# Dense FFN moved from the routed tiles into the attention loop of a fused attention and mixture-of-experts kernel

## The chip, the core and the metric

The kernel runs on one core of one Trainium2 chip. A core has a matrix engine (TensorE, PE in the profile), a vector engine (VectorE, DVE), a scalar engine (ScalarE, ACT), a general engine (GpSimd, POOL) and a synchronising engine (SyncE, SP) that here only issues DMAs. Each engine runs its own instructions in their order and waits on semaphores for the others. Data moves between device memory and the on-chip memory SBUF by DMA; matrix products land in PSUM. The metric is device time in microseconds of one execution.

## The reference

```python
def _attn_ref(q, k, v, g_q, g_k):            # q, k, v: (8, 12, 448, 64)
    q_n, k_n = rmsnorm(q, g_q), rmsnorm(k, g_k)
    scores = (1/8) * q_n @ k_n^T
    attn = softmax(scores)                    # over the last axis
    return attn @ v

def _moe_ref(x, w_gate, w1_dense, w2_dense, w1, w2):   # x: (3584, 768)
    y_dense = maximum(x @ w1_dense, 0) @ w2_dense       # 768 -> 512 -> 768
    logits = x @ w_gate                                 # 8 experts
    e = argmax(logits); gate = softmax(logits)[e]
    y_moe = gate * (maximum(x @ w1[e], 0) @ w2[e])      # one expert per row
    return y_dense + y_moe
```

The attention output of the 8 batches, with its 12 heads side by side, is x: 3584 rows of 768. Every row goes through the dense FFN and through one of eight expert FFNs of the same size.

## The kernel before

The program has two stages and a planning part between them.

**First stage.** It loops over 48 tiles t; a tile is two heads of one batch, so six tiles make a batch. Two tiles make a group g; the q and k of a group are loaded by SP (`load`, L132, three buffers each) and its v by POOL (`load_v`, L140, two buffers, converted to bf16 on the way). For a tile, POOL squares q and k (`sq`, L151), DVE sums the squares (`ssq`, L152), ACT turns a group's sums into factors (L158, L159), DVE multiplies (`y`, L167), PE transposes (L177), DVE copies the transposes out of PSUM (L182, L184), PE makes the scores (L193), ACT takes their exponentials (`ex`, L195, four of them to a tile), PE multiplies with v (`attend`, L206), DVE divides (`divide`, L214, L219), PE transposes the result (L227) and ACT copies it (L229). After a batch's sixth tile `route` (L238 to L259) makes its logits, its one-hot choice and its gate, and SP writes a record of each row to device memory: x in bf16 and the gate. Squares are made four tiles ahead, normalised values three ahead, scores one ahead.

A buffer of q or k is free for the load of group g when the second tile of group g-3 has been multiplied on DVE; so SP's load waits for DVE (L167), POOL's square waits for the load, and DVE's sum waits for POOL.

The weights come by DMAs that POOL issues: two for the dense FFN with group 1 and two for each expert with every second group from the fourth on (`norm_ahead`). DMAs that POOL issues share one queue.

**Planning** (L305 to L390). From the one-hot choices, DVE and PE work out where each row stands when rows are sorted by expert, each expert's rows padded to whole tiles of 128: 35 slot tiles.

**Second stage.** For each slot tile, POOL gathers 128 records by an indirect DMA (L397, two tiles ahead), PE transposes x (L407), multiplies with the expert's w1 (L414) and with the dense w1 (L420), ACT applies the two relus (L416 with the gate, L423), PE transposes the expert's hidden values (L426) and multiplies the dense ones (L432) and the expert's (L436) with their w2 into one PSUM tile, DVE copies it (L440) and POOL scatters 128 rows of 3,072 bytes to the output by an indirect DMA (L441). A scatter waits for the one before it to have landed, since both write the output.

The order on each engine is set by a scheduler that places instructions as it expects them to become ready; the source order is only its input.

Of the kernel before, what the change touches and what calls it, by code (L numbers as in the profile page):

```python
# [8 lines left out]
F32 = mybir.dt.float32  # L9
# [8 lines left out]
def kernel(  # L18
# [86 lines left out]
    xd = nc.dram_tensor("x_rows", (N, RW // 2), F32).ap()  # L105
    oh = const.tile([P, B, 4, E], BF16)
    wgb = const.tile([P, KD, E], BF16)
    nc.gpsimd.dma_start(wgb, moe_w_gate.rearrange("(ko p) e -> p ko e", p=P))
# [4 lines left out]
    def load_weights(dst1, dst2, s1, s2):  # L113
        nc.gpsimd.dma_start(dst1, s1.rearrange("(ko p) f -> p ko f", p=P))
        nc.gpsimd.dma_start(dst2, s2.rearrange("(fo p) d -> p fo d", p=P))

    def load_expert(dst, e):
        load_weights(dst[:, 0].rearrange("p (ko f) -> p ko f", f=F),
                     dst[:, 1].rearrange("p (fo d) -> p fo d", d=Dm), moe_w1[e], moe_w2[e])

    with tc.tile_pool(name="a_ld", bufs=3) as ld, \
         tc.tile_pool(name="a_sb", bufs=2) as sb, \
         tc.tile_pool(name="a_sc", bufs=2, space=bass.MemoryType.PSUM) as scp, \
         tc.tile_pool(name="a_av", bufs=1, space=bass.MemoryType.PSUM) as avp, \
         tc.tile_pool(name="a_tr", bufs=2, space=bass.MemoryType.PSUM) as trp:
        xin, ssqs, rs, xn, qkT, exs, vas, xnats, xTs = {}, {}, {}, {}, {}, {}, {}, {}, {}

        def load(g):
            b, h0 = divmod(g * GP * 2, H)
            for name, src in (("q", q), ("k", k)):  # L130
                t = ld.tile([SC, 2 * GP, JJ * D], F32, tag="x" + name)
                nc.sync.dma_start(  # L132
                    t, src[b, h0:h0 + 2 * GP].rearrange("h (p j) d -> p h (j d)", j=JJ))
                xin[name, g] = t
            ssqs[g] = sb.tile([SC, 2, 2 * GP * JJ], F32, tag="ssq", name="ssq")

        def load_v(g):
            b, h0 = divmod(g * GP * 2, H)
            vr = ld.tile([SC, 2 * GP, JJ * D], BF16, tag="vr", bufs=2)
            nc.gpsimd.dma_start(vr, v[b, h0:h0 + 2 * GP].rearrange("h (p j) d -> p h (j d)", j=JJ))  # L140
            va = ld.tile([SC, 2 * GP, JJ, D + 2], BF16, tag="va")
            nc.vector.memset(va[:, :, :, D:], 1.0)
            nc.vector.tensor_copy(va[:, :, :, :D], vr.rearrange("p h (j d) -> p h j d", d=D))  # L143
            vas[g] = va

        def squares(t):
            g, i = divmod(t, GP)
            for n, name in enumerate("qk"):
# [5 lines left out]
                    sq.rearrange("p h (j d) -> p (h j) d", d=D), AX.X, ALU.add)  # L154

        def rnorm(g):
            r = sb.tile([SC, 2, 2 * GP * JJ], F32, tag="r", name="r")
            nc.scalar.activation(r, ssqs[g], AF.Ln, bias=eps_t[:SC], scale=1.0 / D)  # L158
            nc.scalar.activation(r, r, AF.Exp, scale=-0.5)  # L159
            rs[g] = r  # L160

        def normalise(t):
            g, i = divmod(t, GP)
            for n, name in enumerate("qk"):
# [8 lines left out]
        def transposes(t):  # L173
            for name in "qk":
                ps = trp.tile([P, S], BF16, tag="tr")
                for j in range(JJ):
                    nc.tensor.transpose(ps[:, j * SC:(j + 1) * SC],  # L177
                                        xn[name, t][:, j].rearrange("p h d -> p (h d)"),
                                        ident[:SC, :SC])
                y = sb.tile([P, S], BF16, tag="T" + name)  # L180
                if name == "q":
                    nc.vector.tensor_scalar(y, ps, gqk, None, op0=ALU.mult)  # L182
                else:
                    nc.vector.tensor_copy(y, ps)  # L184
                qkT[name, t] = y
# [296 lines left out]
```

## Time and profile before

| | |
|---|---|
| median of three runs | 606.62 us (598.64, 606.62, 606.91) |
| profiled execution | 599.36 us, span 597.7 us, mean granted TensorE clock 0.838 |
| PE busy | 443.1 us, 74% of the span |
| DVE busy | 311.6 us, 52% |
| ACT busy | 247.4 us, 41% |
| POOL busy | 205.7 us, 34% |
| chain that ended last | DMA 31%, issue 26%, PE 17%, DVE 15% |

The span is from the first to the last instruction. The granted clock is the share of 2.4 GHz that TensorE was given: 1.00 is 2.4 GHz and 0.50 is 1.2 GHz; a mean between them is a mixture. A busy share is an average over stages that have different limits, so the rows below are taken by stage.

### The profile page before, as it was taken

Reading aid. Unit: us, or ns where it says so; the run is one execution under the profiler, and the core shown is the slowest. Engines: PE = TensorE matmul, PEld = TensorE weight load, DVE = VectorE, ACT = ScalarE, POOL = GpSimd, SP = SyncE. Lnnn points to the kernel's source line nnn. Section 1 sums busy time; section 2 is a strip of 40 time slices with the busy share of each in tenths; the row PEclk is TensorE's granted clock in tenths of the full one; section 3 lists DMA queues with packets and bytes.
Section 4 is the critical chain, followed back from the end, with each engine's and each line's share of the span. In section 5 each row is a group of like instructions: output and inputs, shape, how many; then the busy total and the mean of one; then the engine's idle time right before and its main releaser. Section 6 shows DMA issues by size and latency. Waiting matters only on the chain.

```text
span 597.7 us, 11804 instructions
## 1 busy us (share of the span) xinstructions
PE 443.1 (74%) x4682; PEld 294.6 (49%) x4682; DVE 311.6 (52%) x666; ACT 247.4 (41%) x367; POOL 205.7 (34%) x223
## 2 busy tenths in 40 slices
PE   0558766679986697689781058888889888888895
PEld 0335444445554465456450046556656565555663
DVE  4589976678778768776645513223232322223231
ACT  0447774566676677667780002111121122111220
POOL 5567654336344333542000022222322233222321
PEclk9998985575587858855995559999999999999999
DMA  8999999993654365443101012222122122222210
GB/s 174 222 157 237 239 250 225 230 237 80 148 130 125 82 137 139 78 124 78 47 3 47 0 41 82 71 80 80 64 86 91 65 81 93 90 80 73 81 63 1
DMA packets 55253, 65.89 MB, mean 110 GB/s; under 512 B 4365, under 2 KB 51725, under 8 KB 55200
## 3 DMA queue, kind: packets, MB, share of 16 engines
q0 software_dynamic: 28768, 37.59, 30.2%
q1 hardware_dynamic: 26432, 27.54, 16.5%
q8 instruction: 39, 0.64, 0.4%
q14 instruction: 14, 0.11, 0.1%
HBM read 68.27 MB, written 19.28 MB: 146 GB/s over the span
## 4 chain that ended last, share of the span: by engine, by line
DMA 31%; issue 26%; PE 17%; DVE 15%; POOL 4%; ACT 4%; SPq 1%; POOLq 0%; DVEq 0%; ACTq 0%
DMA out_dram<-ys,dest 16%; DMA vr<-in_v_dram 7%; PE av L206 7%; DMA t<-in_k_dram 5%; PE ps L193 5%; DVE y L167 4%; ACT ex L195 4%; POOL sq L151 3%; PE ps L177 2%; DVE xa L219 2%; DMA t<-in_q_dram 2%; DVE ssq L152 2%; PE ps L227 2%; DVE va L143 1%; POOL xg L397 1%
## 5 line engine op out<-in xcount | busy, mean ns | idle before, releaser
L195 ACT ACTIVATE ex<-ps 112x896 bf16<-112x896 f32 x192 | 168.9, 918 | 67.7 <-PE ps L193 66.5
L151 POOL TENSOR_TENSOR sq<-t 112x512 f32<-112x512 f32 x96 | 101.5, 1074 | 109.1 <-DMA t<-in_q_dram 56.3
L193 PE MATMUL ps<-y 64*112 64x448 bf16 x384 | 98.3, 493 | 41.9 <-DVE y L184 25.9
L206 PEld LDWEIGHTS <-ex 112*128 112x128 bf16 x1536 | 73.6, 114 | 70.8 <-issue 40.4
L206 PE MATMUL av<-va,ex 112*128 112x65 bf16 x1536 | 93.8, 220 | 18.1 <-DVE xa L219 18.0
L416 ACT ACTIVATE hs<-he,xg 128x512 bf16<-128x512 f32 x35 | 24.1, 687 | 183.0 <-PE he L414 183.0
L441 POOL DMA_INDIRECT out_dram<-ys,dest x35 | 35.5, 1016 | 158.7 <-DVE ys L440 158.7
L167 DVE TENSOR_TENSOR y<-t,r 112x512 bf16<-112x512 f32 x96 | 78.7, 843 | 1.6 <-ACT r L159 1.6
L152 DVE TENSOR_REDUCE ssq<-sq 112x8 f32<-112x512 f32 x96 | 62.9, 675 | 26.8 <-POOL sq L151 26.8
L440 DVE COPY ys<-yp 128x768 f32<-128x768 f32 x35 | 33.5, 958 | 77.4 <-PE yp L436 77.4
L432 PE MATMUL yp<-wd,hdT 128*128 128x384 bf16 x280 | 51.6, 327 | 25.8 <-ACT hdT L423 20.0
L397 POOL DMA_INDIRECT xg<-x_rows,row x35 | 34.2, 977 | 86.3 <-DVE dest L390 70.6
L193 PEld LDWEIGHTS <-y 64*112 64x112 bf16 x384 | 30.3, 148 | 64.3 <-DVE y L184 29.4
L177 PE MATMUL ps<-ident,y 112*128 112x112 bf16 x384 | 40.1, 262 | 26.9 <-DVE y L167 24.6
L428 DVE COPY heT<-hp 128x512 bf16<-128x512 bf16 x35 | 14.9, 425 | 85.1 <-PE xp L407 71.5
L420 PEld LDWEIGHTS <-wd 128*128 128x128 bf16 x840 | 51.1, 99 | 8.6 <-issue 0.6
L420 PE MATMUL hd<-xT,wd 128*128 128x128 bf16 x840 | 53.9, 222 | 0.0
L414 PE MATMUL he<-we,xT 128*128 x210 | 52.3, 386 | 0.8 <-DVE xT L409 0.8
L436 PE MATMUL yp<-we,heT 128*128 x280 | 51.2, 326 | 0.0
L432 PEld LDWEIGHTS <-hdT 128*128 128x128 bf16 x280 | 24.5, 98 | 45.3 <-ACT hdT L423 24.6
L177 PEld LDWEIGHTS <-y 112*128 112x128 bf16 x384 | 30.1, 124 | 29.7 <-DVE y L167 25.3
L423 ACT ACTIVATE hdT<-hd 128x512 bf16<-128x512 f32 x35 | 20.9, 597 | 43.3 <-PE xp L407 38.9
(95 smaller groups left out, 392.8 us busy)
## 6 DMA issues: line engine op xcount, KB each, us to landing
we<-in_moe_w_dram POOLq DMA_DIRECT2D x16, 768.0 KB, 29.1
t<-in_q_dram SPq DMA_DIRECT2D x24, 448.0 KB, 5.9
t<-in_k_dram SPq DMA_DIRECT2D x24, 448.0 KB, 7.0
vr<-in_v_dram POOLq DMA_DIRECT2D x24, 224.0 KB, 6.7
x_rows<-xa SPq DMA_DIRECT2D x8, 577.5 KB, 3.7
wd<-in_moe_w_dense_dram POOLq DMA_DIRECT2D x2, 768.0 KB, 10.1
x_rows<-xa SPq DMA_DIRECT2D x8, 96.2 KB, 3.6
xg<-x_rows,row POOLq DMA_INDIRECT x35, 3.1
```

The costliest lines, as they stand in the source:

```text
L151: nc.gpsimd.tensor_mul(sq, x, x)
L152: nc.vector.tensor_reduce(ssqs[g][:, n, 2 * i * JJ:(2 * i + 2) * JJ], sq.rearrange("p h (j d) -> p (h j) d", d=D), AX.X, ALU.add)
L167: nc.vector.tensor_mul(y.rearrange("p j h d -> p h j d"), x.rearrange("p h (j d) -> p h j d", d=D), rs[g][:, n, 2 * i * JJ:(2 * i + 2) * J ...
L177: nc.tensor.transpose(ps[:, j * SC:(j + 1) * SC], xn[name, t][:, j].rearrange("p h d -> p (h d)"), ident[:SC, :SC])
L193: nc.tensor.matmul(ps[:, hh, :S], qkT["k", t][d0:d0 + D, j * SC:(j + 1) * SC], qkT["q", t][d0:d0 + D, :], start=True, stop=True)
L195: nc.scalar.activation(exs[t][:, j], ps[:, :, :S], AF.Exp, scale=scale)
L206: nc.tensor.matmul(av[t][:, hh, mi * De:(mi + 1) * De], exs[t][:, j, hh, QC[mi]:QC[mi] + P], vas[t // GP][:, 2 * (pr % GP) + hh, j, :De], ...
L397: nc.gpsimd.indirect_dma_start(out=xg, out_offset=None, in_=xd, in_offset=bass.IndirectOffsetOnAxis(ap=row[:, t:t + 1], axis=0))
L414: nc.tensor.matmul(he, xT[:, kk], we[:, bass.ds(ereg, 1), 0, kk * F:(kk + 1) * F].rearrange("p o f -> p (o f)"), start=(kk == 0), stop=(kk ...
L420: nc.tensor.matmul(hd[:, ff], wd1[:, kk, ff * P:(ff + 1) * P], xT[:, kk], start=(kk == 0), stop=(kk == KD - 1))
L432: nc.tensor.matmul(yp[:, dd, :HD], hdT[:, ff], wd2[:, ff, dd * HD:(dd + 1) * HD], start=(ff == 0), stop=False)
L436: nc.tensor.matmul(yp[:, dd, :HD], heT[:, ff], we[:, bass.ds(ereg, 1), 1, ff * Dm + dd * HD:ff * Dm + (dd + 1) * HD] .rearrange("p o f -> ...
```

## The change

The dense FFN leaves the second stage. A batch's dense FFN runs in the first stage during the next batch's six tiles, cut into 28 pieces (`dense1`: a quarter of the hidden columns in three parts; `dense2`: 112 rows by 384 columns in two parts), spread over 22 of the 24 steps of those tiles. The last batch's pieces have no next batch and follow the loop. `dense2` writes its rows, 112 by 768 in float32, into the record in device memory, so that a record row grows from 1,540 to 4,612 bytes and the gather brings x, gate and dense output together; DVE adds the dense part while it empties PSUM. The slot tiles do only the expert FFN, in a PE order written out by hand in which neighbouring tiles overlap; gathers run four tiles ahead, with five buffers.

Around that, the division is made per head instead of per tile, v has three buffers and is loaded with q and k, the first group's load is split in two, a tile's steps stand in another source order, the four PSUM banks beside the scores are one pool, and the weight loads are a list of 19 of which three are issued ahead of the loop and half an expert every two and a half tiles in it.

```diff
-    xd = nc.dram_tensor("x_rows", (N, RW // 2), F32).ap()
+    RC = RW // 2 + Dm
+    rec = nc.dram_tensor("records", (N, RC), F32).ap()
...
+        def dense1(b, ff, part, n=3):
+            if part == 0:
+                if ff == 0:
+                    hTs[b] = sb.tile([P, FT, S], BF16, tag="hT", name="hT", bufs=1)
+                ffs[0] = wkp.tile([P, S], F32, tag="wk", name="ff")
+            for kk in range(part * KD // n, (part + 1) * KD // n):
+                nc.tensor.matmul(ffs[0], wd1[:, kk, ff * P:(ff + 1) * P], xTs[b][:, kk],
+                                 start=(kk == 0), stop=(kk == KD - 1))
+            if part == n - 1:
+                nc.scalar.activation(hTs[b][:, ff], ffs[0], AF.Relu)
+
+        def dense2(b, j, dd, part, n=2):
+            if part == 0:
+                if dd == 0:
+                    ffs[1] = sb.tile([SC, 2, Dm // 2], F32, tag="ys", name="ys")
+                ffs[0] = wkp.tile([SC, Dm // 2], F32, tag="wk", name="ff")
+            for ff in range(part * FT // n, (part + 1) * FT // n):
+                nc.tensor.matmul(ffs[0], hTs[b][:, ff, j * SC:(j + 1) * SC],
+                                 wd2[:, ff, dd * Dm // 2:(dd + 1) * Dm // 2],
+                                 start=(ff == 0), stop=(ff == FT - 1))
+            if part == n - 1:
+                if dd == 0:
+                    nc.scalar.copy(ffs[1][:, dd], ffs[0])
+                else:
+                    nc.vector.tensor_copy(ffs[1][:, dd], ffs[0])
+                    r0 = b * S + j * SC
+                    nc.sync.dma_start(rec[r0:r0 + SC, RW // 2:],
+                                      ffs[1].rearrange("p a d -> p (a d)"))
...
+        for t in range(NT + NPR):
+            if t < NT:
+                if t % GP == 0:
+                    load(t // GP + 3)
+                while nw < len(wjobs) and (nw - 2) * 5 <= t * 2:
+                    nc.gpsimd.dma_start(*wjobs[nw])
+                    nw += 1
+            for i in range(4):
+                if t + 1 < NT:
+                    scores(t + 1, i)
+                if i % 2 == 0:
+                    if t + 2 < NT:
+                        transposes(t + 2, "qk"[i // 2])
+                    if i == 2 and 0 < t <= NT:
+                        xtrans(t - 1)
+                elif t < NT:
+                    attend(t, i // 2)
+                dense(t, i)
+                if i < 2:
+                    if t + 2 * GP < NT:
+                        squares(t + 2 * GP, "qk"[i])
+                elif t + 3 < NT:
+                    normalise(t + 3, "qk"[i - 2])
+                if i == 3 and t % GP == GP - 1 and t + 1 < NT:
+                    values((t + 1) // GP)
...
-            nc.vector.tensor_copy(ys, yp[:, :, :HD])
+            nc.vector.tensor_add(ys, yp[:, :, :HD],
+                                 xgs[t][:, RW // 2:].rearrange("p (a d) -> p a d", a=2))
...
+        with tc.manual_schedule(engines={mybir.EngineType.PE}):
+            for t in range(2):
+                xtrans(t)
+            gemm1(0)
+            htrans(0)
+            for t in range(NTL):
+                if t + 4 < NTL:
+                    gather(t + 4)
+                if t + 1 < NTL:
+                    gemm1(t + 1)
+                if t + 2 < NTL:
+                    xtrans(t + 2)
+                gemm2(t)
+                if t + 1 < NTL:
+                    htrans(t + 1)
```

`xtrans` transposes a slot tile's x, `gemm1` is the expert's first product with the relu on ACT, `htrans` the transposes of its hidden values with the copy on ACT, `gemm2` the second product with the add and the scatter.

What the change does to the order on an engine is shown at three places.

DVE before, in the later half of the first stage: from the last multiplication of a group (`y`, L167), which frees its buffers, to the first sum of squares of the group that is loaded into them (`ssq`, L152).

```order
L167 TENSOR_TENSOR y<-t,r 112x2x4x64 x2
L152 TENSOR_REDUCE ssq<-sq 112x8 x2
L182 TENSOR_SCALAR y<-ps,gqk 128x448
L184 COPY y<-ps 128x448
L214 RECIPROCAL inv<-av 128x8
L167 TENSOR_TENSOR y<-t,r 112x2x4x64
L219 TENSOR_TENSOR xa<-av,inv 128x2x4x64
L167 TENSOR_TENSOR y<-t,r 112x2x4x64
L152 TENSOR_REDUCE ssq<-sq 112x8 x2
```

And DVE now, at such a place (L173 is the multiplication, L158 the sum of squares, L215 and L217 the division, L283 the copy of dense output):

```order
L173 TENSOR_TENSOR y<-xk,r 112x2x4x64
L215 RECIPROCAL inv<-av 128x4
L147 MEMSET va 112x16x2
L148 COPY va<-vr 112x16x64
L217 TENSOR_TENSOR xa<-av,inv 128x4x64
L283 COPY ys<-ff 112x384
L187 TENSOR_SCALAR y<-tr,gqk 128x448
L173 TENSOR_TENSOR y<-xq,r 112x2x4x64
L215 RECIPROCAL inv<-av 128x4
L158 TENSOR_REDUCE ssq<-sq 112x8
```

In both pieces eight instructions stand between the two. Before, from group 11 on (groups counted from 0, to 23), seven to ten stand there at two groups of three and fifteen at the third. Now there are eleven and five at groups 14 and 15, and seven or eight at each one after them; at the groups before 14, from 23 to 38 stand there.

SP before, in the same part of the stage: a batch's record rows stand between loads.

```order
L132 DMA t<-in_q_dram 112x4x256
L132 DMA t<-in_k_dram 112x4x256
L258 DMA x_rows<-xa 128x3x385
L259 DMA x_rows<-xa 64x385
L132 DMA t<-in_q_dram 112x4x256
```

And SP now (L137 the loads, L255 and L256 the rows of x, L285 the dense rows):

```order
L137 DMA xk<-in_k_dram 112x4x256
L285 DMA records<-ys 112x768 x2
L137 DMA xq<-in_q_dram 112x4x256
L285 DMA records<-ys 112x768
L137 DMA xk<-in_k_dram 112x4x256
L285 DMA records<-ys 112x768
L255 DMA records<-xa 128x3x385
L256 DMA records<-xa 64x385
```

Four writes of dense rows per batch came into SP's order, and in four of the seven batches one of them stands between the q load and the k load of one group.

POOL now, in the first third of the stage: half an expert's weights (L320), squares (L157) and a load of v (L141).

```order
L320 DMA we<-in_moe_w_dram 128x4x768
L157 TENSOR_TENSOR sq<-xq 112x512
L157 TENSOR_TENSOR sq<-xk 112x512
L320 DMA we<-in_moe_w_dram 128x6x512
L141 DMA vr<-in_v_dram 112x4x256
L157 TENSOR_TENSOR sq<-xq 112x512
```

Here the scheduler undid the new spacing: all sixteen halves stand ahead of the squares of tile 15, as in the kernel before they all stood ahead of the squares of tile 17 (tiles counted from 0).

## Rows read from the trace of the kernel before

**Rows 1.** Cores: the span, and the mean granted clock.

```profile
core 0: 597.7 us, clock 0.838
```

**Rows 2.** Windows: length, then PE, PEld, DVE, ACT, POOL busy; clock, DMA share, GB/s.

```profile
23.00:135.00 112.00, 79.28 (x888) 50.13 (x888) 85.81 (x172) 70.75 (x106) 61.44 (x65) 0.78 1.14 225
135.00:285.00 150.00, 122.36 (x1396) 80.05 (x1395) 113.35 (x254) 105.31 (x154) 61.91 (x63) 0.67 0.49 112
285.00:315.00 30.00, 23.02 (x371) 15.54 (x370) 16.00 (x42) 24.07 (x35) 0.00 (x0) 1.00 0.08 25
315.00:352.00 37.00, 4.24 (x53) 3.50 (x53) 17.55 (x46) 0.47 (x2) 2.57 (x3) 0.50 0.08 25
363.00:592.00 229.00, 201.99 (x1896) 137.02 (x1894) 65.47 (x102) 43.67 (x68) 64.83 (x65) 1.00 0.23 76
```

**Rows 3.** The source line L195 in three stretches: count, duration, first and last start.

```profile
L195 ACT ACTIVATE ex<-ps x70: 898/917/948, 23.6 to 135.8; 112x896 bf16<-112x896 f32 x70
...
L195 ACT ACTIVATE ex<-ps x99: 899/917/942, 135.8 to 284.3; 112x896 bf16<-112x896 f32 x99
...
L195 ACT ACTIVATE ex<-ps x25: 909/918/953, 284.3 to 310.8; 112x896 bf16<-112x896 f32 x25
```

**Rows 4.** Chain that ended last, 240 to 253 us: start, length, what.

```profile
240.52 0.69 DVE ssq L152
...
244.62 6.50 DMA t<-in_k_dram
...
251.26 1.05 POOL sq L151
...
252.33 0.69 DVE ssq L152
```

**Rows 5.** DMA issues: count, size of one, median time from issue to landing.

```profile
we<-in_moe_w_dram POOLq DMA_DIRECT2D x16, 768.0 KB, 29.1
```

**Rows 6.** Windows of 15 us in the first stage, columns as in rows 2.

```profile
270.00:285.00 15.00, 14.32 (x134) 9.12 (x133) 9.55 (x22) 10.53 (x16) 4.08 (x4) 0.53 0.33 76
285.00:300.00 15.00, 11.37 (x182) 7.48 (x182) 9.97 (x29) 12.26 (x19) 0.00 (x0) 1.00 0.14 47
```

**Rows 7.** Lines by form: total busy, mean ns of one, idle before, releaser.

```profile
L440 DVE COPY ys<-yp 128x768 f32<-128x768 f32 x35 | 33.5, 958 | 77.4 <-PE yp L436 77.4
...
L219 DVE TENSOR_TENSOR xa<-av,inv 128x512 bf16<-128x512 f32 x48 | 32.6, 679 | 0.2
...
L229 ACT COPY xT<-ps 128x448 bf16<-128x448 bf16 x48 | 25.7, 536 | 27.8 <-PE ps L227 27.2
...
L423 ACT ACTIVATE hdT<-hd 128x512 bf16<-128x512 f32 x35 | 20.9, 597 | 43.3 <-PE xp L407 38.9 <-PE hd L420 4.4
```

**Rows 8.** Timeline of one slot tile: start, length, instruction, idle before and releaser.

```profile
457.97 1.02 POOL L441 DMA_INDIRECT out_dram<-ys,dest  x1 [3.33 <-DVE ys L440]
...
459.17 0.39 PE L426 MATMUL hp<-ident,hs 128*128 128x128 bf16 x4
...
459.29 0.98 POOL L397 DMA_INDIRECT xg<-x_rows,row  x1 [0.30 <-issue]
...
459.39 0.50 PE L407 MATMUL xp<-ident,xg 128*128 128x128 bf16 x6
...
460.70 1.47 PE L432 MATMUL yp<-wd,hdT 128*128 128x384 bf16 x8 [0.81 <-ACT hdT L423]
...
462.01 1.46 PE L436 MATMUL yp<-we,heT 128*128 x8
...
463.31 1.46 PE L414 MATMUL he<-we,xT 128*128 x6
...
464.61 1.50 PE L420 MATMUL hd<-xT,wd 128*128 128x128 bf16 x24
```

**Rows 9.** The source line L441 from 360 us on: its scatters, and landing.

```profile
L441 POOL DMA_INDIRECT out_dram<-ys,dest x35: 982/1017/1037, 363.7 to 592.0; - x35
...
DMA to landing us min/median/max: 2.1/3.1/3.1
```

More of the change, by code (lines that the diff above doesn't have):

```diff
@@ L171, in normalise, with transposes @@
                 xn[name, t] = y
[L173 to L185, printed above, removed]
+        def transposes(t, name):
+            ps = wkp.tile([P, S], BF16, tag="wk", name="tr")
+            for j in range(JJ):
+                nc.tensor.transpose(ps[:, j * SC:(j + 1) * SC],
+                                    xn[name, t][:, j].rearrange("p h d -> p (h d)"),
+                                    ident[:SC, :SC])
+            y = sb.tile([P, S], BF16, tag="T" + name)
+            if name == "q":
+                nc.vector.tensor_scalar(y, ps, gqk, None, op0=ALU.mult)
+            else:
+                nc.vector.tensor_copy(y, ps)
+            qkT[name, t] = y
         def scores(t, j):
             if j == 0:
-                exs[t] = sb.tile([SC, JJ, 2, S], BF16, tag="ex", name="ex", bufs=2)
+                exs[t] = sb.tile([SC, JJ, 2, S], BF16, tag="ex", name="ex")
             ps = scp.tile([SC, 2, 512], F32, tag="sc")
@@ L233, in route @@
         def route(b):
-            lp = trp.tile([P, 4, E], F32, tag="tr")
+            lp = wkp.tile([P, 4, E], F32, tag="wk", name="tr")
             for mi in range(4):
@@ new lines, with dense @@
+        ffs = [None, None]
+        PIECES = [(dense1, ff, p) for ff in range(FT) for p in range(3)] + \
+                 [(dense2, j, dd, p) for j in range(JJ) for dd in range(2) for p in range(2)]
+        NSL = 4 * NPR - 2
+        def dense(t, i):
+            b, pr = divmod(t, NPR)
+            n = 4 * pr + i - 2
+            if b > 0 and n >= 0:
+                for f, *args in PIECES[n * len(PIECES) // NSL:(n + 1) * len(PIECES) // NSL]:
+                    f(b - 1, *args)
+        for g in range(3):
+            load(g)
@@ L275 @@
+        for job in wjobs[:3]:
+            nc.gpsimd.dma_start(*job)
         for t in range(2 * GP):
-            norm_ahead(t)
+            squares(t)
+        values(0)
         for t in range(3):
@@ L422, in ffn @@
-            hdT = sb.tile([P, FT, P], BF16, tag="hdT")
-            nc.scalar.activation(hdT, hd, AF.Relu)
-            hp = ps1.tile([P, FT, P], BF16, tag="tr")
-            for ff in range(FT):
-                nc.tensor.transpose(hp[:, ff], hs[:, ff * P:(ff + 1) * P], ident)
-            heT = sb.tile([P, FT, P], BF16, tag="heT")
-            nc.vector.tensor_copy(heT, hp)
+                nc.tensor.matmul(he, xTs[t][:, kk],
+                                 we[:, bass.ds(eregs[t], 1), 0, kk * F:(kk + 1) * F]
+                                 .rearrange("p o f -> p (o f)"),
+                                 start=(kk == 0), stop=(kk == KD - 1))
@@ L429, in ffn, with htrans, gemm2 @@
+            hes[t] = sb.tile([P, F], BF16, tag="hs", name="hs")
+            nc.scalar.activation(hes[t], he, AF.Relu, scale=gate)
+        def htrans(t):
+            hp = psh.tile([P, FT, P], BF16, tag="hp")
+            for ff in range(FT):
+                nc.tensor.transpose(hp[:, ff], hes[t][:, ff * P:(ff + 1) * P], ident)
+            heTs[t] = sb.tile([P, FT, P], BF16, tag="heT", name="heT")
+            nc.scalar.copy(heTs[t], hp)
+        def gemm2(t):
             yp = psy.tile([P, 2, 512], F32, tag="y")
```

186 lines of the change are left out of this document (76 added, 110 removed).

## The prediction

> **What bounds the kernel now.** I read the cores first, for the time to be explained: a span of 597.7 us [rows 1], in an execution of 599.36 us. That is at the lower of the two levels of the three runs shown (598.64, and 606.62 and 606.91); the sum below is made against 599.4, and the median of 606.62 stands 1.2% above it. A difference under 2% is no change here.
>
> Then the windows by stage [rows 2]. The first stage is three stretches. From 23 to 135 us the DMA engines are saturated (share 1.14, 225 GB/s): the sixteen halves of the experts' weights take 29.1 us each to land [rows 5]. From 135 to 285 us the DMA share is 0.49 and no engine is full: DVE is busy 113 of 150 us, PE 122 at a mean clock of 0.67. In the last 30 us nothing is loaded any more. After planning, the second stage has PE busy 202 of 229 us at clock 1.00.
>
> The exponentials count tiles, four to each [rows 3]: 17.5 tiles in the first 112 us, 24.75 tiles in the next 148.5 us (6.0 us each), 6.25 tiles in the last 26.5 us (4.2 us each). What holds the middle stretch is seen in the chain [rows 4]: sum of squares, then 4.1 us of DVE work up to the multiplication that frees a buffer, then 6.50 us of load into it, 1.05 us of square, and the next sum. The two sums stand 11.81 us apart, and that is one group, or 5.9 us a tile: a loop through the load. TensorE is a second limit of the same size: a tile has 56 matmuls (8 scores, 32 with v, 12 transposes, 4 for the gate on average), so 134 matmuls in 15 us at clock 0.53 are 2.4 tiles of 6.0 us, and 182 at clock 1.00 are 3.25 tiles of 3.5 us busy [rows 6].
>
> In the second stage 34 periods lie between the first and the last scatter, 6.71 us each [rows 9]. PE fills them, except for 0.81 us behind the dense relu [rows 8].
>
> **The change, part by part.**
>
> *Second stage.* The dense products (24 and 8 matmuls) and the wait of 0.81 us go. From start to start, the expert's second product takes 1.30 us, its first 1.30, four transposes 0.22, and six of them by that 0.33 [rows 8]: 3.15 us a tile. Three other things then come close. A scatter waits for the one before it: 3.1 us to land [rows 9] and 0.30 us until POOL goes on [rows 8], 3.4 us. POOL itself needs 1.02 + 0.98 + 2 x 0.30 = 2.6 us. The DMA engines carry 128 x (4,612 + 3,072) bytes = 0.98 MB a tile: at the 225 GB/s of the saturated stretch 4.4 us, at what share 0.23 for 76 GB/s makes of a full share (330 GB/s) 3.0 us [rows 2]. So the period lies between 3.4 and 4.4 us; I take 3.6, near the scatters' loop, since large rows of one queue resemble this stage's own DMAs more than the cast weights. 228.3 - 34 x 3.6 = 105.9 us saved; the first scatter comes about 1 us later, since two tiles' x are transposed first: **-105**. The add in place of the copy keeps DVE at about 0.96 us, the new ACT copy costs at most the 0.60 us of the relu that goes [rows 7]; both lie under 3.15 us of PE.
>
> [...] A batch has 24 x 448 + 32 x 384 = 23,040 columns: 9.8 us, or 1.64 us a tile, and double at half clock. So a tile needs 5.1 us of PE at 2.4 GHz and 9.2 us at 1.2 GHz [rows 6].
>
> *Dense pieces elsewhere.* To a batch, ACT gets four relus of about 0.54 us and four copies of about 0.48 [rows 7], 0.68 us a tile; with 105.3 / 24.75 = 4.26 [rows 2, 3] it is 4.9. DVE gets four copies of half of the 0.96 us one [rows 7], 0.3 us a tile, and the division in two halves, 0.2 us at most in fixed cost beside the 0.68 of the whole; with 113.4 / 24.75 = 4.58 it is 5.1. So three engines stand at about 5 us, where DVE, ACT and PE were at 4.6, 4.3 and 3.5.
>
> *Saturated stretch.* The weights still stand early in POOL's queue, and v queues behind them. New there are the dense rows of one batch, 448 x 3,072 bytes = 1.38 MB at 225 GB/s [rows 2]: **+6**. The earlier issue of v is costed at nothing: its cover is the saturation itself, since the same bytes have to come.
>
> *The 30.5 tiles after it.* 175 us before [rows 3]. About 6.5 tiles, whose loads have 23 or more DVE instructions of lead, run at the old 6.0 us. For some 20 tiles the order puts the sum of squares seven or eight DVE instructions after the release, at every group now. The load loop then is 6.50 + 1.05 + 0.16 us [rows 4], and DVE work that I count, by the instructions between, at 4.6 us plus 0.3 for routing and dense copies: 12.6 us a group, 6.3 a tile. The last four tiles, without loads, take about 5.3 (the engines' 5.1, where 4.2 stood over 4.3). 39 + 126 + 21 = 186: **+11**. A dense row's write that SP meets between q and k waits for DVE; I leave it to a rival.
>
> *Clock.* PE was 95% busy for 15 us at clock 0.53 [rows 6], so being busy alone did not raise it here; and over the middle stretch 0.67 means two thirds of the time at 1.2 GHz [rows 2]. Each share s of those 30.5 tiles at 9.2 instead of 6.3 us costs s x 89 us. At the low end s is 0; at the high end it is the old two thirds (+59). The nearest row for a stream with full-array products is the second stage, at 1.00 throughout; the nearest for one that waits on loads is the middle stretch. I take a fifth, nearer the first since 1.64 us of every 5.1 are such products: **+18**. The Trainium skill ("TensorE: Matmul & The Clock Gate", section "Why this matters for your kernels") says that an engine kept busy is granted the full clock; this case's trace, with 0.53 at 95% busy, does not agree. By that rule the term would be 0 and the sum 522.
>
> *Last batch.* Its dense FFN has nothing beside it and stands ahead of planning: 9.8 us at the clock of 1.00 that the end of the stage had [rows 2], 19.6 at half: **+11**. Planning itself, with PE nearly idle from 315 to 352 us [rows 2], is unchanged.
>
> The sum: 599.4 - 105 + 6 + 11 + 18 + 11 = **540 us**.
>
> **The rivals.**
>
> *The first stage hides everything.* The load loop doesn't bind, the clock stays at 1.00 and the 30.5 tiles take 5.3 us, 162 instead of 175; the last batch 10, the scatters' loop 3.4 (-113). 599.4 + 6 - 13 + 10 - 113 = 490 us. For it: ACT and DVE have room at 5.1. Against it: rows 4 are a loop that no engine's speed shortens.
>
> *The DMA engines become the bound of the second stage.* 4.4 us a tile instead of 3.6: 27 us more, 567. For it: 0.98 MB a tile instead of 0.59, and 25 MB more in all (3,584 rows written and 4,480 gathered, of 3,072 bytes). Against it: the share was only 0.23 [rows 2]. The Trainium skill ("DMA: Bandwidth & Descriptors", section "Issuing engines are not separate DMA queues") says that all DMAs run on the same 16 engines whoever issues them, which speaks against moving more; that 768 KB took 29.1 us to land in the saturated stretch [rows 2, 5] agrees with it.
>
> *SP's queue.* The dense rows stand among the loads; one that waits for a late piece holds the load behind it. If each of the last ten groups loses 3 us so, 30 us: 570. For it: the loop has no slack there. Against it: most writes stand behind both loads of a group.
>
> *TensorE stays at 1.2 GHz, and the kernel is slower.* Then the dense pieces cost double just where PE was already full: 11.5 tiles of the saturated stretch and the 30.5 after it at 9.2 us. The first stretch takes 6 x 6.4 + 106 = 144 instead of 112 (+32), the rest 281 instead of 175 (+106), the last batch 20: 599.4 + 32 + 106 + 20 - 105 = 652 us. It decides against the change from about two thirds of those tiles at half clock on, the very share that the middle stretch has now. Against it: at 1.2 GHz the stream would be unbroken and a third of it full-array products, and in the second stage such a stream had 1.00.
>
> That the pieces don't stand among the attention is excluded by the order.
>
> **How the numbers follow.** The forecast has a chance of 0.47, everything hidden 0.2, DMA 0.12, SP's queue 0.11, half clock 0.1. The time is that of the likeliest: **540 us**. Its own range, from the clock's term between 0 and +40 and the period between 3.4 and 3.8, is 515 to 569. The range from 490 to 588 leaves out half of "everything hidden" and nearly all of the half-clock case: about 2 in 10. Faster by over 2% is under 587: the forecast and three rivals, less their tails, 0.85; within 2% 0.07, from the tails of SP's queue and of a clock that is half for much of the time; slower 0.08.
>
> **What would show it.** Right: periods of 3.4 to 3.8 us between scatters, DVE still waiting for squares in the later half of the first stage, PE clock above 0.85 there, one stretch of dense products alone ahead of planning. Wrong: clock near 0.5 with PE full in the first stage; scatters that land later than 3.1 us; DVE without waits and tiles near 5.2 us; loads on SP that start long after their release.

## The result, and the profile after

The changed kernel takes **531.19 us** (median of four runs, 528.78 to 533.24), the kernel before 606.76 in the runs beside them (598.64 to 610.52): a ratio of **0.879, 95% interval 0.869 to 0.890**. The profiled execution took 529.39 us with a span of 527.3, against 599.36 and 597.7 before [rows 1]. So 70.4 us of span went, where the forecast had 59.4 go (540.0 us).

First the windows by stage, columns as in [rows 2]:

```profile
23.00:135.00 112.00, 91.56 (x937) 52.45 (x938) 86.20 (x199) 72.44 (x111) 54.79 (x58) 0.85 1.16 237
135.00:285.00 150.00, 133.50 (x1592) 76.29 (x1590) 123.59 (x318) 113.89 (x184) 65.93 (x65) 0.96 0.61 149
285.00:315.00 30.00, 30.00 (x375) 17.40 (x374) 20.64 (x61) 26.46 (x40) 0.00 (x0) 1.00 0.22 70
...
380.00:527.00 147.00, 111.90 (x778) 63.54 (x790) 50.68 (x67) 42.14 (x67) 64.78 (x65) 0.97 0.60 196
```

The granted clock of the middle stretch is 0.96 where it was 0.67. TensorE, which filled the second stage before, is busy 112 of 147 us there now: something else sets its pace. The exponentials, four to a tile, as in [rows 3]:

```profile
L200 ACT ACTIVATE ex<-ps x65: 897/917/956, 27.9 to 133.8; 112x896 bf16<-112x896 f32 x65
...
L200 ACT ACTIVATE ex<-ps x98: 898/918/1003, 133.8 to 283.2; 112x896 bf16<-112x896 f32 x98
...
L200 ACT ACTIVATE ex<-ps x30: 898/917/942, 285.2 to 322.5; 112x896 bf16<-112x896 f32 x30
```

The middle stretch holds 98 exponentials, 24.5 tiles in 149.4 us: 6.1 us a tile with dense products among them, 6.0 before. The last one comes at 322.5 instead of 310.8 us. Then the scatters, which answer to [rows 9]:

```profile
L486 POOL DMA_INDIRECT out_dram<-ys,dest x35: 985/1022/1042, 380.5 to 521.9; - x35
...
DMA to landing us min/median/max: 3.1/3.6/5.3
```

Thirty-four periods in 141.4 us are 4.16 us each, where 6.71 stood. POOL's own timeline shows what such a period is made of (start, length, instruction, idle before it and releaser):

```profile
406.26 1.02 POOL L486 DMA_INDIRECT out_dram<-ys,dest  x1 [2.16 <-DMA out_dram<-ys,dest]
407.58 0.97 POOL L440 DMA_INDIRECT xg<-records,row  x1 [0.30 <-issue]
410.14 1.02 POOL L486 DMA_INDIRECT out_dram<-ys,dest  x1 [1.59 <-DMA out_dram<-ys,dest]
411.47 0.97 POOL L440 DMA_INDIRECT xg<-records,row  x1 [0.30 <-issue]
414.03 1.02 POOL L486 DMA_INDIRECT out_dram<-ys,dest  x1 [1.59 <-DMA out_dram<-ys,dest]
```

A scatter that waits for nothing but the one before it starts 3.88 us after it: 1.02 + 0.30 + 0.97 of POOL, and 1.59 until that one has landed. Some fourteen of the 34 periods have this length. Five are over 5 us; in the longest of them whose wait the trace names, POOL stands 3.85 us until the scatter before has landed.

Last, DVE between the stages:

```profile
329.28 0.09 DVE L348 MEMSET oh<- 64x32 uint32 x1
...
337.12 0.56 DVE L283 COPY ys<-ff 112x384 f32<-112x384 f32 x1 [1.65 <-DMA records<-ys]
...
338.93 0.56 DVE L283 COPY ys<-ff 112x384 f32<-112x384 f32 x1 [1.26 <-DMA records<-ys]
...
342.43 0.42 DVE L355 COPY tot<-tp 128x256 f32<-128x256 f32 x1 [2.93 <-DMA records<-ys]
```

The routing is done at 329.3, and planning's first copy runs at 342.4. The last batch's dense products lie between, and behind them three waits of DVE for dense rows to be written.

Where the 70.4 us went, by the profiled executions of the two kernels:

| stretch | before | after | difference |
|---|---|---|---|
| to the first exponential | 23.6 | 27.9 | +4.3 |
| first to last exponential | 287.2 | 294.6 | +7.4 |
| to planning's first copy (`tot`) | 10.6 | 19.9 | +9.3 |
| to the first transposed slot tile | 30.6 | 25.5 | -5.1 |
| to the first scatter | 11.7 | 12.5 | +0.9 |
| 34 periods | 228.3 | 141.4 | -86.9 |
| behind the last scatter | 5.7 | 5.4 | -0.3 |

### The profile page after: what moved, and what is told of

It is laid out like the page before. It is cut to its first block, busy times and chain, and to the rows that moved or that the text cites. A ratio compares the mean times of both kernels' runs of the same rounds, so it can differ in the third digit from the quotient of the medians.

```text
span 527.3 us, 10720 instructions
## 1 busy us (share of the span) xinstructions
PE 400.9 (76%) x3995; PEld 231.9 (44%) x4010; DVE 320.1 (61%) x759; ACT 272.7 (52%) x431; POOL 207.4 (39%) x223
## 3 DMA queue, kind: packets, MB, share of 16 engines
q1 hardware_dynamic: 30560, 38.56, 25.5%
## 5 line engine op out<-in xcount | busy, mean ns | idle before, releaser
L211 PE MATMUL av<-va,ex 112*128 112x65 bf16 x1536 | 73.5, 202 | 16.8 <-DVE xa L217 15.5
L157 POOL TENSOR_TENSOR sq<-xq 112x512 f32<-112x512 f32 x48 | 53.8, 1120 | 82.3 <-DMA xq<-in_q_dram 39.3
L158 DVE TENSOR_REDUCE ssq<-sq 112x8 f32<-112x512 f32 x96 | 64.0, 672 | 30.3 <-POOL sq L157 30.3
L440 POOL DMA_INDIRECT xg<-records,row x35 | 34.0, 970 | 90.4 <-DVE dest L433 80.0
L276 PE MATMUL ff<-wd,hT 128*112 128x384 bf16 x256 | 62.8, 357 | 8.0 <-DVE xa L217 4.9
L157 POOL TENSOR_TENSOR sq<-xk 112x512 f32<-112x512 f32 x48 | 51.4, 1071 | 31.4 <-DMA xk<-in_k_dram 15.2
L182 PE MATMUL tr<-ident,y 112*128 112x112 bf16 x384 | 38.8, 229 | 26.3 <-DVE y L173 25.8
L472 ACT COPY heT<-hp 128x512 bf16<-128x512 bf16 x35 | 20.5, 586 | 68.1 <-PE hp L470 68.1
L265 PE MATMUL ff<-xT,wd 128*128 128x448 bf16 x192 | 50.3, 362 | 4.0 <-DVE xa L217 3.8
L484 DVE TENSOR_TENSOR ys<-yp,xg 128x768 f32<-128x768 f32 x35 | 33.5, 958 | 29.3 <-PE yp L478 29.3
L173 DVE TENSOR_TENSOR y<-xq,r 112x512 bf16<-112x512 f32 x48 | 42.2, 880 | 0.2 <-ACT r L164 0.2
```

Source lines behind the costliest of these rows:

```text
L157: nc.gpsimd.tensor_mul(sq, x, x)
L158: nc.vector.tensor_reduce(ssqs[g][:, n, 2 * i * JJ:(2 * i + 2) * JJ], sq.rearrange("p h (j d) -> p (h j) d", d=D), AX.X, ALU.add)
L173: nc.vector.tensor_mul(y.rearrange("p j h d -> p h j d"), x.rearrange("p h (j d) -> p h j d", d=D), rs[g][:, n, 2 * i * JJ:(2 * i + 2) * J ...
L182: nc.tensor.transpose(ps[:, j * SC:(j + 1) * SC], xn[name, t][:, j].rearrange("p h d -> p (h d)"), ident[:SC, :SC])
L211: nc.tensor.matmul(av[:, mi], exs[t][:, j, hh, QC[mi]:QC[mi] + P], vas[t // GP][:, 2 * (t % GP) + hh, j, :De], start=(j == 0), stop=(j == ...
L265: nc.tensor.matmul(ffs[0], wd1[:, kk, ff * P:(ff + 1) * P], xTs[b][:, kk], start=(kk == 0), stop=(kk == KD - 1))
```

## The experiments

Twelve kernels ran, on four chips: deep, narrow, nodense and half on one; slots, alt, noload and plan on another; control, plan3 and fine on a third; unread on a fourth. On these chips the kernel before took 577 to 592 us and not 599 to 611, while the changed kernel (control) took 530.8 us, about the same as at first. So the ratio of 0.879 is that of the first runs; beside control it is 0.914. Why the kernel before depends on the chip is not shown, since it has only one profile; I compare the changed kernel's relatives with each other. Narrow, nodense, half, slots, alt, noload, plan and unread are single runs.

### The second stage: which loop makes 4.16 us

**deep**: gathers seven tiles ahead.

```diff
-            xg = sb.tile([P, RC], F32, tag="xg", name="xg")
+            xg = sb.tile([P, RC], F32, tag="xg", name="xg", bufs=8)
...
-                if t + 4 < NTL:
-                    gather(t + 4)
+                if t + 7 < NTL:
+                    gather(t + 7)
```

> Changed kernel with xg in 8 buffers instead of 5 and gathers issued seven tiles ahead instead of four; nothing else. In the changed kernel's second stage a scatter comes every 4.16 us. Theory G (the loop through a gather's landing): a gather lands 7.8 us after POOL issued it, and scatter (1.3 us) + gather (1.0) + landing (7.8) + four us of transposes, second product and add come to some 12.5 us for three tiles. With six tiles for the same chain it is 2.1 us a tile, so the period falls to that of the next limit, 3.4 to 3.9 us, and the time by 9 to 26 us, to 503 to 520. Theory B (bytes on one queue or on the 16 engines): the same 0.98 MB a tile have to pass, gathers only land later, the period stays above 4.0 and the time at 526 to 533. Theory C (a scatter waits for the one before to land, 3.6 us + 0.3): 3.9 us, 520.

Measured: 525.97 us (525.31 to 526.50), periods of 4.11 us (378.8 to 518.5). TensorE did wait for gathers in the changed kernel (21.6 us between 390 and 520 us, by the list of waits), but seven tiles of lead in place of four take hardly anything off the period: theory G falls. The period above 4.0 us and the time are what theory B forecast, and theory C's 3.9 us is missed, so this run alone doesn't decide between those two; the next two do.

**narrow**: records of x and gate alone.

```diff
-    RC = RW // 2 + Dm
+    RC = RW // 2
...
-            nc.vector.tensor_add(ys, yp[:, :, :HD],
-                                 xgs[t][:, RW // 2:].rearrange("p (a d) -> p a d", a=2))
+            nc.vector.tensor_copy(ys, yp[:, :, :HD])
```

> Changed kernel with records of x and gate alone (1,540 bytes): the dense rows go to a tensor of their own that nobody gathers, and the add is a copy; so the dense part is left out of the output. 0.39 MB less a tile. Theory G (gather's landing): it lands in 4 to 5 us instead of 7.8, the loop falls to about 3.2 us a tile, period 3.3 to 3.9 by the scatters. Theory B (bytes): 0.59 MB instead of 0.98, period down to PE's 3.2 to 3.5. Theory C (scatter waits for scatter): 3.9 us or a bit under, as a scatter's bytes are unchanged. First stage unchanged within 2 us.

Measured: 522.33 us, periods of 3.92 us (381.8 to 515.2). With 0.59 MB a tile instead of 0.98 only 0.2 us go, where theory B had the period fall to 3.2 to 3.5. The 3.92 is what theory C expects, and it sits on the 3.88 of the timeline above.

**alt**: every second scatter to another tensor, on top of deep.

```diff
-                out=out, out_offset=bass.IndirectOffsetOnAxis(ap=dest[:, t:t + 1], axis=0),
+                out=out if t % 2 else out2, out_offset=bass.IndirectOffsetOnAxis(ap=dest[:, t:t + 1], axis=0),
```

> As the kernel with gathers seven ahead, but every second scatter goes to another tensor of the same shape (so half of the output's rows are left out); bytes, instructions and queue are the same, only a scatter no longer has to wait for the one right before it. Theory C (a scatter's own loop, 3.88 us from start to start when it ends last): the period falls from 4.11 to 3.2 to 3.5, TensorE's 3.15 being next, and the time by 20 to 30 us against the kernel with gathers seven ahead. Theory Q (the queue or the DMA engines serve the transfers no faster): the period stays at 3.8 or more and gathers or scatters land later.

Measured: 496.25 us. Its scatters, and a window of its second stage:

```profile
L487 POOL DMA_INDIRECT evens<-ys,dest x18: 982/1022/1042, 381.6 to 488.7; - x18
L487 POOL DMA_INDIRECT out_dram<-ys,dest x17: 982/1022/1032, 384.7 to 486.2; - x17
```

```profile
390.00:485.00 95.00, 94.60 (x714) 57.61 (x712) 44.73 (x59) 38.20 (x60) 53.92 (x55) 1.00 0.80 265
```

Thirty-four periods in 107.1 us: 3.15 us, TensorE busy 94.6 of 95 us, and the same bytes at 265 GB/s. Single scatters land later than in the changed kernel (a median of 5.4 to 5.5 us from 390 to 485 us), as theory Q had it, and the period falls all the same, since the next one no longer waits for them. This decides it: the pace was set by a scatter waiting for the scatter right before it, not by the DMA engines, the queue or the gathers. The Trainium skill ("DMA: Bandwidth & Descriptors", section "Issuing engines are not separate DMA queues") has all transfers share 16 engines; here they were not full, at a share of 0.60 with the chain and 0.80 without it.

**slots**: the pipelined stage, with the dense FFN back in it and none in the first stage.

```diff
+        def densef(t):
+            hd = psh.tile([P, FT, P], F32, tag="hd")
+            for ff in range(FT):
+                for kk in range(KD):
+                    nc.tensor.matmul(hd[:, ff], wd1[:, kk, ff * P:(ff + 1) * P], xTs[t][:, kk],
...
+                    nc.tensor.matmul(yp[:, dd, :HD], hdTs[t][:, ff],
+                                     wd2[:, ff, dd * HD:(dd + 1) * HD],
...
                     gemm1(t + 1)
+                    densef(t + 1)
```

> The pipelined second stage with the dense FFN back in it: 24 dense products behind the expert's first six, 8 ahead of the expert's second eight, in the same PSUM; records of x and gate alone, no dense pieces in the first stage. So the two halves of the change come apart. Theory W (work counts): TensorE needs 3.15 + 2 x 1.31 = 5.8 us a tile, which is then the period instead of 3.9 (the kernel without any dense product), 34 x 1.9 = 65 us more than that one's 471: 534, and the first stage ends at 284 us. The pipelining alone then gives most of the gain, and the move to the first stage some 10 us more. Rival (the slots have room): the tile's 0.8 us of waiting takes half of it, period 5.0, 508 us, and then the move to the first stage was a loss.

Measured: 545.75 us, where the kernel before took 590.69 beside it; periods of 5.72 us. TensorE's timeline of one tile:

```profile
435.38 1.46 PE L460 MATMUL he<-we,xT 128*128 x6
436.67 1.50 PE L471 MATMUL hd<-xT,wd 128*128 128x128 bf16 x24
438.01 0.50 PE L451 MATMUL xp<-ident,xg 128*128 128x128 bf16 x6
438.35 1.46 PE L487 MATMUL yp<-wd,hdT 128*128 128x384 bf16 x8
439.65 1.46 PE L492 MATMUL yp<-we,heT 128*128 x8
440.95 0.39 PE L479 MATMUL hp<-ident,hs 128*128 128x128 bf16 x4
441.17 1.46 PE L460 MATMUL he<-we,xT 128*128 x6
```

No row has an idle time before it: 5.79 us from start to start, the sum of the work (theory W). The total is 12 us over what I expected, 9 of them in the first stage, whose clock was 0.70 in this run. The pipeline (with the reordered first stage) thus gives 45 us on this chip, and the move of the dense products some 15 more, the latter across chips (545.75 against control's 530.82). Those 15 are uncertain: the same first stage took 9 us less in nodense, below.

### The first stage: clock and loop

**nodense**: narrow without any dense product.

```diff
-            if b > 0 and n >= 0:
+            if False:
```

> As the kernel with narrow records, and without any dense product in the first stage: the dense FFN is left out altogether. Theory F (the full-array products hold TensorE's clock): the granted clock between 135 and 285 us falls from 0.96 back to about 0.67, as in the kernel before, and a tile takes 5.9 to 6.2 us there all the same, so the dense pieces were nearly free. Theory L (the clock came from the loop's new order, not from the products): the clock stays above 0.9 and a tile takes 5.2 to 5.9 us, as ACT, DVE and PE are relieved. By both the stretch of dense products ahead of planning (some 11 us) is gone.

Measured: 471.06 us, 51 under narrow on the same chip. The last exponential comes at 283.8 us instead of 324.6: dense products cost 41 us in the first stage, and the rest behind it. Its window and its exponentials:

```profile
135.00:285.00 150.00, 127.94 (x1659) 83.89 (x1660) 129.95 (x351) 123.74 (x181) 61.47 (x64) 0.80 0.50 113
```

```profile
L201 ACT ACTIVATE ex<-ps x119: 898/917/1002, 134.0 to 283.8; 112x896 bf16<-112x896 f32 x119
```

A tile takes 5.04 us, with DVE busy 130 of 150 us: less than even theory L's 5.2. The clock, 0.80, lies between the two theories; in slots, which has the same first stage, a tile takes 5.3 us at 0.70. So without dense products the new loop takes some 0.7 to 1 us less for a tile than the kernel before, on other chips.

The dense products were not free, but nodense takes away more than their work. DVE's waits for squares between 135 and 285 us (in all, times, longest) are this row in control, the changed kernel on another chip:

```profile
DVE ssq L158 <- POOL sq L157: 21.2, 24, 2.9
```

In unread, a run further down that has the products but waits for no load, they are this one:

```profile
DVE ssq L167 <- POOL sq L166: 0.5, 1, 0.5
```

In nodense the list has no such wait; the largest of DVE's waits there is this one:

```profile
DVE inv L216 <- PE av L212: 11.7, 16, 1.6
```

In DVE's order in nodense, from 36 to 43 instructions stand between the release of a buffer and the sum of squares that needs it, from group 11 on, where in the changed kernel at most eleven do from group 14 on. So the scheduler, with the dense pieces among its instructions, closed the loop through the load again. Unread's last exponential comes at 305.8 us, between nodense's 283.8 and narrow's 324.6. By that, an estimate across chips, about half of the 41 us is the products' work and about half is the wait that came with them.

**half**: dense products on 64 rows of the array.

```diff
-                nc.tensor.matmul(ffs[0], wd1[:, kk, ff * P:(ff + 1) * P], xTs[b][:, kk],
+                nc.tensor.matmul(ffs[0], wd1[:D, kk, ff * P:(ff + 1) * P], xTs[b][:D, kk],
...
-                nc.tensor.matmul(ffs[0], hTs[b][:, ff, j * SC:(j + 1) * SC],
-                                 wd2[:, ff, dd * Dm // 2:(dd + 1) * Dm // 2],
+                nc.tensor.matmul(ffs[0], hTs[b][:D, ff, j * SC:(j + 1) * SC],
+                                 wd2[:D, ff, dd * Dm // 2:(dd + 1) * Dm // 2],
```

> Changed kernel whose dense products use 64 of the 128 rows of the array (half of the contraction is left out, so the dense part is wrong); columns, instructions and waits are the same. Theory F in its narrow form (it is full rows that hold the clock): the granted clock between 135 and 285 us falls below 0.85, and the first stage gets 10 to 60 us longer. Rival (it is the columns that stream without a pause, however many rows): the clock stays at 0.93 or more and the time at 526 to 535 us.

Measured: 635.77 us, slower than the kernel before on that chip (585). The window:

```profile
135.00:285.00 150.00, 150.00 (x1129) 85.59 (x1126) 95.12 (x227) 86.24 (x131) 47.52 (x48) 0.50 0.42 103
```

TensorE is busy for all 150 us, and at 1.2 GHz throughout. The last exponential comes at 414.0 us, 92 us later than in the changed kernel and beyond the 10 to 60 us that I expected. Same instructions, same columns, half the rows: in this kernel the clock depends on the rows that the dense products use. With the same products on 128 rows, deep and narrow had 0.97 and 0.96 on the same chip. Without any dense product it was 0.80 (nodense), with TensorE busy 128 of 150 us. In the nine profiled executions with full dense products and all loads the middle stretch had 0.96 to 1.00. The Trainium skill ("TensorE: Matmul & The Clock Gate", section "Why this matters for your kernels") asks for an engine that is kept busy; this window, busy without a gap at 0.50, does not agree.

**noload** and **unread**: q and k loaded for the first groups alone; and loaded at the old moments, into buffers that nobody waits for.

```diff
+            if g >= 3:
+                for name in "qk":
+                    xin[name, g] = xin[name, g - 3]
```

```diff
+                    xin[name, g] = xin[name, 0]
+                    dm[name, g] = ld.tile([SC, 2 * GP, JJ * D], F32, tag="x" + name,
+                                          name="x" + name, bufs=2)
...
+                    nc.vector.tensor_tensor(scr, dm[name, g + 1][:, 0, :1], xn["k", t][:, 0, 0, :1],
+                                            ALU.mult)
```

> Changed kernel in which q and k are loaded for the first three groups of tiles alone and used again by all later ones (so most of the attention's inputs are left out); v is loaded as before. Theory L (the loop through the load sets the 6.1 us a tile between 135 and 285 us): a tile takes 5.1 to 5.5 us there and the last exponential of the first stage comes 20 us or more earlier. Theory P (TensorE, busy 89%, with the dense products among the rest, sets it): 5.8 us or more, and less than 10 us in all.

> Changed kernel in which all tiles use the q and k of the first group, while every later group's q and k are still loaded, each when the buffer before was released as in the changed kernel (a one-column product on DVE reads the buffer behind the last multiplication of a group), into buffers that no square and no multiplication reads. So the bytes, their queue and their moment stay, and only the wait for them goes (most of the attention's inputs are left out of the result). Theory L (the loop: release, load, square, sum): nearly all of what leaving the loads out gave stays, a tile between 134 and 285 us takes 5.5 to 5.7 us instead of 6.1, and the last exponential comes at 295 to 303 us instead of 322. Theory B (the bytes of q and k, 0.92 MB a group, slow the other transfers and through them the stage): 5.9 us or more and the last exponential at 314 us or later.

Measured: 502.21 and 511.41 us; 5.52 and 5.64 us a tile; last exponential at 295.4 and 305.8 us. Of unread, the exponentials and the window:

```profile
L214 ACT ACTIVATE ex<-ps x107: 897/917/952, 133.8 to 284.8; 112x896 bf16<-112x896 f32 x107
```

```profile
135.00:285.00 150.00, 138.73 (x1711) 80.79 (x1709) 141.64 (x366) 122.32 (x197) 60.39 (x62) 0.99 0.64 156
```

With the bytes kept and the wait gone (DVE waits 0.5 us for squares, by the row shown with nodense) DVE is busy 142 of 150 us instead of 124: the loop through the load is what held the tile at 6.1 us (theory L), and DVE is the next limit. The last exponential misses the 303 us of theory L by 3 us, and stays far from theory B's 314. Of the 29 us that noload gave, unread keeps 20; the bytes explain at most the other 9, across chips.

### Better versions

**plan**, **control** and **plan3**: planning ahead of the last batch's dense products on TensorE, written into the first stage's loop, so that the scheduler places both together. To make room, q, k and v move to a pool that closes before planning opens its own; control is the changed kernel itself.

```diff
                     if i == 2 and 0 < t <= NT:
                         xtrans(t - 1)
+                    if i == 2 and t == NT:
+                        one = ones_.enter_context(tc.tile_pool(name="m_one", bufs=1))
+                        nc.vector.memset(oh[:D, :, 3, :], 0.0)
+                        ohf = oh.rearrange("p b m e -> p (b m e)")
+                        cp = wkp.tile([P, NC4, E], F32, tag="wk", name="tr")
...
-                if dd == 0:
+                if dd == 0 or b == B - 1:
```

> Changed kernel in which the planning (counts, positions and the two sums on TensorE ahead of them) stands right behind the last batch's routing, ahead of that batch's dense products in program order, and the last sum of planning behind them; the last batch's dense copies are all ACT's. Theory D (the last batch's dense products cost their whole time, 11 us, because nothing stands beside them): the first transposed tile comes 32 to 36 us after the last exponential instead of 45.5, and the time falls by 9 to 13 us. Rival (planning on DVE is disturbed, or the products run at half clock among its pauses): 0 to 5 us.

> The changed kernel itself, unaltered, on the chip and in the rounds of the two that follow, so that these can be set against it: some 515 to 533 us, 0.87 to 0.92 of the kernel before.

> The kernel with the last batch's dense products behind the planning's first sums, again, timed beside the changed kernel. Theory D: 9 to 13 us under the changed kernel of the same chip. Rival: less than 5 us under it.

Measured: plan 514.16 us. Timed together, plan3 513.09 (512.23 to 515.00) and control 530.82 (529.49 to 534.60): 17.7 us less. Against the kernel before plan3 stands at 0.882 (0.876 to 0.889), and control at 0.914 (0.906 to 0.922). TensorE of plan3 between the stages:

```profile
326.18 0.27 PE L338 MATMUL tr<-oh,tri 128*128 128x256 bf16 x1 [1.42 <-DVE oh L335]
326.29 0.27 PE L340 MATMUL tr<-oh,ones 128*128 128x256 bf16 x1
326.40 4.70 PE L267 MATMUL ff<-xT,wd 128*128 128x448 bf16 x24
330.94 5.55 PE L278 MATMUL ff<-wd,hT 128*112 128x384 bf16 x32
342.25 2.99 PE L412 MATMUL tr<-val,sel 128*128 128x105 bf16 x32 [5.76 <-issue]
```

DVE plans while TensorE does 10.1 us of dense products, and planning's first copy follows the routing's last step by 0.65 us (325.95 to 326.60) instead of 13.1. The 12.5 us that go there are what theory D had, the three waits for written dense rows among them; the first transposed tile comes 32.8 us after the last exponential, in control 45.7. Most of the rest of the 17.7 lies elsewhere: the last exponential comes 2.6 us earlier than in control and the first scatter stands 1.2 us nearer to the first transposed tile. What made that is not shown.

**fine**: on top of plan, q and k in six buffers of one tile.

```diff
+        def loadx(t):
...
+                xin[name, t] = xl.tile([SC, 2, JJ * D], F32, tag="x" + name, name="x" + name, bufs=XB)
...
             if t < NT:
+                loadx(t + XB)
                 if t % GP == 0:
                     load(t // GP + 3)
```

> The kernel with the last batch's dense products during planning, and q and k in six buffers of one tile each instead of three of two tiles (same bytes of SBUF), loaded tile by tile as each is released; the sum of squares then stands 36 to 50 DVE instructions behind the release of its buffer through most of the middle stretch, where it stood 6 to 12 behind. Theory L (the loop through the load sets the time of a tile): a good part of what leaving the loads out gave comes back, 8 to 20 us, and a tile between 135 and 285 us takes 5.5 to 5.8 us. Rival (it was the bytes of q and k on the DMA engines, or the smaller transfers land no sooner): within 4 us of the kernel without this edit.

Measured: 517.05 us (515.74 to 519.14), 4 us more than plan3. Two windows:

```profile
165.00:195.00 30.00, 26.55 (x331) 15.66 (x332) 29.80 (x73) 23.87 (x40) 14.40 (x15) 1.00 0.62 149
195.00:225.00 30.00, 24.83 (x287) 14.01 (x285) 22.22 (x57) 22.96 (x37) 13.45 (x13) 1.00 0.56 143
```

Up to 195 us DVE is full; then it waits again, and by the order from about the thirtieth tile on only 6 to 17 DVE instructions stand between a buffer's release and the sum, not the 36 to 50 that I expected for most of the stretch. DVE still waits 16.6 us for squares between 135 and 285 us, in plan3 18.4. So the time is as the rival has it, but the edit did not take the loop away, and the run can't speak for the rival's cause or against theory L.

plan3 is the fastest kernel here that computes everything. Alt, which leaves out half of the output's rows, says that up to 30 us more lie in the chain of scatters; a version that writes all rows to one tensor without that wait was not tried, since the rows of two scatters are kept apart by nothing but their indices.

## Why the prediction was right, and where not

It was right in sign, range and mechanism of most steps; two large errors of opposite sign, 19 us too much saved in the second stage and 28 us too much lost in the first, nearly cancelled. That 531 lies so near to 540 is partly luck.

*Second stage, -105: mis-sized, -86.9 + 0.9.* The step that failed is "A scatter waits for the one before it: 3.1 us to land and 0.30 us until POOL goes on, 3.4 us." The loop is the right one, as alt shows. But its measured length is 3.88 us, and 4.16 with periods of 5 to 6 us among them. I composed it from a landing time and a pause, in a stage where no scatter waited for the last; from start to start it is half a microsecond more, also in narrow, whose landing has the same median of 3.1. In the changed kernel the median is 3.6, which I had named as a sign of being wrong. A usual period of 3.4 to 3.8, which I had named as a sign of being right, did not come. Why single scatters land late (up to 5.3 us) stays open: the changed kernel has five periods over 5 us, narrow one, alt none.

*DMA engines as the bound (rival, 4.4 us).* Its number came nearer to 4.16 than mine, and its mechanism is wrong: narrow and alt.

*TensorE's share, 3.15 us a tile*, is what alt ran at.

*Saturated stretch +6, later tiles +11, clock +18: together +35, measured +7.4.* The loop through the load was there and its 6.3 us a tile measured 6.1 (unread takes it away), though its load landed in 5.5 us (the median for k) and not 6.50. The clock's term is mis-sized: I took a fifth of the tiles at 1.2 GHz, and a mean of 0.96 leaves less than a tenth of the stretch there, some 7 us by the same price. The three terms weren't measured one by one. My reason for the low side (full-array products among the rest) was right, and half shows it; I gave it too little weight. The rule of the Trainium skill that I set against the row, a term of 0, came out nearer, for a reason that half speaks against.

*Half clock (rival, 652 us).* Half is this rival made real: 635.8, slower than before, on a chip where the kernel before took 585. The price was near; in the changed kernel the condition did not arise.

*First stage hides everything (rival, 490).* It did not: the loop bound (unread), and nodense shows that the products, with the wait that came with them, cost 41 us there. That the stage grew by only 7.4 us is because the new loop without them is 23 us (slots) to 31 us (nodense) shorter than before, from first to last exponential and across chips. I had no term for that: I added the products to the old loop and priced the order at a small loss.

*Last batch +11: measured +9.3* beside a kernel before that waited 4.2 us at the same place for x rows to be written; plan3 gives its full price, 12.5 us at that place.

*Planning unchanged:* not quite, -5.1. Before, TensorE started the sum of planning 6.6 us after its last input, with no wait shown; after, at once. What that was stays open, as do the 4.3 us ahead of the first exponential.

*SP's queue (rival, 570):* no. Between 135 and 285 us the loads are issued within 0.5 us of the multiplication that frees their buffer; one pair of rows, DVE's and then SP's:

```profile
187.14 0.68 DVE L173 TENSOR_TENSOR y<-xk,r 112x512 bf16<-112x512 f32 x1
...
187.89 0.33 SPq L137 DMA_DIRECT2D xk<-in_k_dram  x1
```

## What to carry to other kernels

Find the chain of a DMA that writes one tensor again and again: its usual period, from start to start in a stretch where it does wait, limits what pipelining can give, and has to be measured there rather than composed from landing times elsewhere. Work that is spread among another stage can change that stage's clock: here to 0.96 from 0.70 to 0.80 with products on 128 rows, and to 0.50 with products on 64. It can also change the scheduler's order: after adding work, count again what stands between a buffer's release and the instruction that needs the next load. And a piece moved ahead of planning cost its whole time here until planning's own work on DVE was started first.

## What the runs showed of the hardware that was not expected

TensorE ran 150 us without a gap at 1.2 GHz with dense products on 64 rows, and the same stretch at a mean clock of 0.96 with 128. The same first-stage code without dense products had 0.80 on one chip and 0.70 on another (nodense and slots). Scatters and gathers together moved 265 GB/s once no scatter waited for the one right before (alt, 390 to 485 us), against 207 in the changed kernel (390 to 520 us).
